# Attention and a max-of-three MLP on one core: DVE takes over the first weight conversions, the hidden layer is split batch by batch, and the queues of the first loads change

## The chip, the cores and the metric

The kernel runs on one core of a Trainium2 chip. Five engines work side by side, each through its own queue of instructions in order: TensorE (PE, with its weight loads, PEld, shown apart), VectorE (DVE), ScalarE (ACT), GpSimd (POOL) and SyncE (SP, which here only issues DMAs). They meet through semaphores. The metric is the device time of one execution in microseconds, and the time of a kernel is the median of its runs.

## What is computed

Twelve heads of attention with a soft cap on the scores, for four batches of 448 tokens, and after it a layer with a maximum over three products:

```python
scores = q @ k.T / sqrt(64)                 # (4, 12, 448, 64) each
scores = cap * tanh(scores / cap)
attn = exp(scores - max); attn = attn / (sum(attn) + 1e-9)
x = heads side by side of attn @ v          # (1792, 768)
h = maximum(maximum(x @ w1, x @ w2), x @ w3)
out = h @ w_out                             # weights 768 x 768, given in 64 bits
```

## The kernel before

**Attention.** The 48 pairs of batch and head go in twelve steps t = 0 to 11 of four heads each (two PE row halves by two column halves). A step has seven key blocks j. For each j, `scores(t, j)` is four products on PE into one of two PSUM tiles `qk`, `tanh(t, j)` (ACT, from PSUM to one of ten tiles `e_t`) and `expo(t, j)` (ACT, in place) follow, `add(t, j)` sums the exponentials on DVE into `s_t`, and `values(t, j)` multiplies by v on PE into `av`. At the start of step t + 1, `sums(t)` adds over the keys by a product with ones on PE into `sm`, `recip(t)` transposes, inverts and transposes back on DVE, `normalize(t)` multiplies `av` by the result on DVE, which frees `av` for `values(t + 1, 0)`, and `split_x(t)` writes x as a high part `xh` and a rest `xl`, both float32r. The two `qk` tiles are used in turn, so `scores(t + 1, 2)` waits until `tanh(t + 1, 0)` has read its tile. In steps 0 to 3 and 11 (`BY_PE`) the last block's exponentials are added by a second product in `sums`, in the others by `add(t, 6)` on DVE.

**Weights.** `conv(n, i)` makes weight tile n (128 x 768, of 24) from its 64-bit form `wd` in steps i: a scaled copy of the upper word on ACT, three integer operations on DVE over `cw`, a cast to `wh` on ACT and the rest to `wl` on DVE. `CONV` says after which attention step which parts stand; they are written between `scores(t + 1, 1)` and `expo(t, 6)`.

**The layer.** `products(n, b, ...)` is eighteen products, `xh wh`, `xl wh`, `xh wl` for six blocks. Eight of the 96 groups (n, b) are done inside attention, one in each of steps 4 to 11 (`FILL`), ahead of `scores(t, 5)`. The other 88 run in `mlp` after it: n = 0 to 17 give the three products of each hidden block, `empty` copies the first to `m_t` (ACT) and takes the maximum with the others (DVE); n = 18 to 23 are the output, copied by ACT and sent by SP. Between n = 17 and n = 18, `split_h(b, f)` writes h as high part and rest over `xh` and `xl`: a cast on ACT and a subtraction on DVE for each of 24 pairs (b, f).

The order on every engine is the order of the code (`tc.manual_schedule()`); waits come from the tiles.

Of the kernel before, what the change touches and what calls it, by code (L numbers as in the profile page):

```python
# [31 lines left out]
CONV = {0: [(0, k) for k in range(5)], 1: [(1, 0), (1, 1)], 2: [(1, 2), (1, 3), (1, 4)],  # L32
        4: [(2, 0), (2, 1)], 5: [(2, 2), (2, 3), (2, 4)], 9: [(3, 0)], 10: [(3, 1)], 11: [(3, 2)]}
FIRST_CONV = 3
# [3 lines left out]
def attn_max_mlp_kernel(ctx: ExitStack, tc: tile.TileContext, q, k, v, cap, wts, out):  # L38
# [28 lines left out]
    r_t = ring("r_t", 2, [128, 2 * QB])  # L67
    xh = ring("xh", B, [128, KC, S], F32R)
# [124 lines left out]
    def conv(n, step):  # L193
# [3 lines left out]
        if step == 0:  # L197
            nc.scalar.activation(out=d, in_=top.bitcast(F32), func=AF.Copy, scale=2.0 ** -112)
            nc.vector.tensor_scalar(
                out=w, in0=w, scalar1=3, scalar2=1, op0=ALU.logical_shift_left, op1=ALU.bitwise_or  # L200
            )
        elif step == 1:
# [3 lines left out]
        elif step == 2:  # L206
# [3 lines left out]
        elif step == 3:  # L210
            nc.scalar.copy(out=h, in_=d)  # L211
        else:
            tt(nc.vector, l, d, h.bitcast(F32), ALU.subtract)
# [10 lines left out]
    def empty(n, b, ps):  # L224
        if n >= 3 * KC:
            o = o_t[outs[0] % len(o_t)]
            outs[0] += 1
            nc.scalar.copy(out=o, in_=ps)
            nc.sync.dma_start(out=out[n - 3 * KC, b], in_=o)
            return  # L230
# [12 lines left out]
    def step(t, eps):  # L243
        last = t - 1
        if t:
            sums(last, last in BY_PE)
            recip(last, eps)
            values(last, 3)
        if t < NG:
            tanh(t, 1)  # L250
            expo(t, 0)
            scores(t, 3)
# [3 lines left out]
        if t < NG:  # L256
            tanh(t, 2)
            expo(t, 1)
            add(t, 1)
            scores(t, 4)  # L260
# [3 lines left out]
        if t < NG:  # L264
            tanh(t, 3)
            expo(t, 2)
            add(t, 2)
# [69 lines left out]
    def mlp(done, convs):  # L337
# [14 lines left out]
        if fast:  # L352
# [6 lines left out]
            for n in range(2):  # L359
# [124 lines left out]
```

## Time and profile before

| | us |
|---|---|
| median of 3 runs (lowest, highest) | 559.41 (553.05, 559.76) |
| profiled execution, its own time | 559.23 |
| profiled execution, span from first to last instruction | 557.2 |
| PE busy in the span | 518.9 |
| DVE busy | 257.9 |
| ACT busy | 235.2 |

The time of the profiled execution is 2.0 us more than its span. A matmul counts as busy from its issue to its end and the next starts before that, so a busy PE may still be paced by something. DVE and ACT are busiest in the first part, the attention, which ends near 213 us; from there PE runs one stream of products. "idle before" in a row is what the engine waited just ahead of it, and the arrow names what ended the wait.

### The profile page before, as it was taken

The page shows a single profiled execution, that of the slowest core. Times are in us where ns is not written, and L with a number is a line of the kernel's source. Part 1 is how long each engine was busy: PE and PEld are TensorE (multiplying, and loading weights), DVE is VectorE, ACT ScalarE, POOL GpSimd, SP SyncE. Part 2 cuts the span into 40 slices and gives each one's busy share as a digit, 9 for nine tenths or more (in the row PEclk, how much of TensorE's full clock was granted, in tenths as well). Part 3 has the DMA queues.
Part 4 walks back from the last instruction along what each step waited for, and adds up shares of the span by engine and source line. Part 5 has one row for each costly group of instructions (what it writes and reads, how often), then busy time and mean ns, then how long its engine had stood idle before and what let it go on. Part 6 is the DMA issues. An engine that isn't in the chain of part 4 may idle for free.

```text
span 557.2 us, 7444 instructions
## 1 busy us (share of the span) xinstructions
PE 518.9 (93%) x3217; PEld 383.8 (69%) x3217; DVE 257.9 (46%) x325; ACT 235.2 (42%) x291; POOL 1.1 (0%) x7
## 2 busy tenths in 40 slices
PE   6598699899999999999999999999999978999997
PEld 2133234454444447999999999999999957999996
DVE  1578577867677884513323323332332366211200
ACT  5788698768978870311121031020111172222211
POOL 0000000000000000000000000000000000000000
PEclk9899899989999999999999999999999986999999
DMA  7322043213243201111111111020130100333111
GB/s 250 127 86 85 31 156 100 100 34 100 72 151 101 89 1 58 58 56 58 56 58 56 58 56 43 27 102 0 58 101 13 58 0 34 107 122 124 67 51 70
DMA packets 12311, 41.44 MB, mean 74 GB/s; under 512 B 1392, under 2 KB 4592, under 8 KB 12272
## 3 DMA queue, kind: packets, MB, share of 16 engines
q1 hardware_dynamic: 12240, 40.90, 21.5%
q8 instruction: 27, 0.44, 0.3%
q14 instruction: 12, 0.10, 0.1%
q0 software_dynamic: 32, 0.00, 0.0%
HBM read 35.39 MB, written 5.51 MB: 73 GB/s over the span
## 4 chain that ended last, share of the span: by engine, by line
PE 80%; ACT 12%; DVE 5%; issue 1%; ACTq 0%; DVEq 0%
PE qk L219 10%; PE qk L218 10%; PE qk L220 10%; PE sm L218 7%; PE qk L117 7%; PE sm L220 7%; PE sm L219 7%; ACT e_t L123 6%; PE av L131 6%; PE av L218 5%; PE av L220 5%; ACT e_t L126 5%; PE av L219 5%; PE sm L145 3%; DVE xl L95 2%; DVE s_t L95 1%
## 5 line engine op out<-in xcount | busy, mean ns | idle before, releaser
L219 PE MATMUL qk<-xl,wh 128*128 128x448 f32 x264 | 99.8, 378 | 6.0 <-DVE xl L95 6.0
L117 PE MATMUL qk<-q_t,k_t 64*64 64x448 f32 x672 | 81.8, 560 | 25.1 <-ACT e_t L123 24.7
L220 PE MATMUL qk<-xh,wl 128*128 128x448 f32 x264 | 98.9, 375 | 0.0
L218 PE MATMUL qk<-xh,wh 128*128 128x448 f32 x264 | 98.9, 375 | 0.0
L123 ACT ACTIVATE e_t<-qk,sc_t 128x896 f32<-128x896 f32 x84 | 83.0, 1002 | 23.2 <-PE qk L117 22.1
L126 ACT ACTIVATE e_t<-e_t,acap 128x896 f32<-128x896 f32 x84 | 86.3, 1038 | 0.4
L211 ACT CAST wh<-cw 128x768 fp32r<-128x768 f32 x24 | 20.0, 834 | 136.4 <-DVE cw L207 136.4
L131 PE MATMUL av<-e_t,v_t 64*64 64x448 f32 x672 | 75.9, 538 | 1.4 <-DVE x_t L95 1.4
L117 PEld LDWEIGHTS qk<-q_t,k_t 64*64 64x64 f32 x672 | 23.3, 135 | 67.8 <-ACT e_t L123 40.9
L218 PE MATMUL sm<-xh,wh 128*128 128x448 f32 x180 | 67.0, 372 | 0.0
L220 PE MATMUL sm<-xh,wl 128*128 128x448 f32 x180 | 66.2, 368 | 0.0
L219 PE MATMUL sm<-xl,wh 128*128 128x448 f32 x180 | 66.1, 367 | 0.0
L95 DVE TENSOR_TENSOR s_t<-s_t,e_t 128x896 f32<-128x896 f32 x55 | 59.9, 1088 | 11.5 <-ACT e_t L126 10.0
L219 PEld LDWEIGHTS qk<-xl,wh 128*128 128x128 f32 x264 | 50.5, 191 | 14.0 <-DVE xl L95 9.2
L218 PEld LDWEIGHTS qk<-xh,wh 128*128 128x128 f32 x264 | 50.8, 193 | 6.0 <-issue 0.7
L220 PEld LDWEIGHTS qk<-xh,wl 128*128 128x128 f32 x264 | 50.7, 192 | 5.1
L131 PEld LDWEIGHTS av<-e_t,v_t 64*64 64x64 f32 x672 | 25.5, 134 | 40.5 <-issue 36.8
L218 PE MATMUL av<-xh,wh 128*128 128x448 f32 x132 | 48.6, 368 | 0.0
L219 PE MATMUL av<-xl,wh 128*128 128x448 f32 x132 | 48.6, 368 | 0.0
L220 PE MATMUL av<-xh,wl 128*128 128x448 f32 x132 | 48.6, 368 | 0.0
L95 DVE TENSOR_TENSOR wl<-cw,wh 128x768 fp32r<-128x768 f32 x24 | 22.9, 955 | 51.3 <-ACT wh L211 51.3
L218 PEld LDWEIGHTS sm<-xh,wh 128*128 128x128 f32 x180 | 33.8, 188 | 8.8 <-DVE s_t L95 5.6
(62 smaller groups left out, 417.3 us busy)
## 6 DMA issues: line engine op xcount, KB each, us to landing
wd<-in_wts_dram SPq DMA_DIRECT2D x24, 768.0 KB, 4.4
q_t<-in_q_dram SPq DMA_DIRECT2D x12, 448.0 KB, 4.3
v_t<-in_v_dram SPq DMA_DIRECT2D x12, 448.0 KB, 3.2
k_t<-in_k_dram SPq DMA_DIRECT2D x11, 448.0 KB, 3.4
out_dram<-q_t SPq DMA_DIRECT2D x8, 224.0 KB, 2.0
out_dram<-s_t SPq DMA_DIRECT2D x8, 224.0 KB, 1.9
out_dram<-x_t SPq DMA_DIRECT2D x8, 224.0 KB, 2.2
k_t<-in_k_dram SPq DMA_DIRECT2D x1, 320.0 KB, 6.5
```

The source lines that it names most:

```text
L95: eng.tensor_tensor(out=out, in0=in0, in1=in1, op=op)
L117: nc.tensor.matmul(ps[rows(s), R, 0:S], k_t[t % 2][rows(R), j, s, :], q_t[t % 2][rows(R), s, :], start=True, stop=True, skip_group_check=True,
L123: nc.scalar.activation(out=e_of(t, j), in_=slot(t, j)[:, :, 0:S], func=AF.Tanh, scale=sc_t)
L126: nc.scalar.activation(out=e_of(t, j), in_=e_of(t, j), func=AF.Exp, scale=acap)
L131: nc.tensor.matmul(av[rows(R), s, 0:S], v_t[t % 2][rows(s), j, R, :], e_of(t, j)[rows(s), R, :], start=(j == 0), stop=(j == NJ - 1), skip_ ...
L145: nc.tensor.matmul(sm[rows(R), s, 0:S], ones[rows(s), :], part[rows(s), R, :], start=(i == 0), stop=(i == len(parts) - 1), skip_group_chec ...
L211: nc.scalar.copy(out=h, in_=d)
L218: nc.tensor.matmul(ps, w_h, a_h, start=(kc == 0), stop=False)
L219: nc.tensor.matmul(ps, w_h, a_l, start=False, stop=False)
L220: nc.tensor.matmul(ps, w_l, a_h, start=False, stop=(kc == KC - 1))
```

## The change

Six edits. (1) `conv` has six steps: the scaled copy and the first integer operation are now separate. In steps 0 and 4 of it the engine is DVE, unless `by_act` is set; tile 0, tile 1 and the cast of tile 2 go to DVE, tile 2's and tile 3's scaled copies stay on ACT (`SCALED`), and all tiles of `mlp` keep ACT. Tile 0's first four parts stand behind single adds of step 0; the other parts are spread over steps 1 to 5, 9 and 10, and stand behind all adds of their step. (2) `values(t, 3)` moves from behind `sums(t)` to ahead of `scores(t + 1, 2)`; in steps without a fill, `scores(t, 6)` comes ahead of `values(t, 0)`. (3) `split_h` is done for batch b right behind group (17, b). (4) The first q load and cap go to ACT's queue, cap from POOL's. (5) The last output tile is emptied in two halves, by DVE and ACT, and sent by SP and ACT. (6) A tile `pad` of 128 bytes per partition stands ahead of x and the weights and moves them. The loads of q and k stand earlier in their step and those of `wd` inside the steps; SP's queue keeps the order of q, k and v.

```diff
-CONV = {0: [(0, k) for k in range(5)], 1: [(1, 0), (1, 1)], 2: [(1, 2), (1, 3), (1, 4)],
-        4: [(2, 0), (2, 1)], 5: [(2, 2), (2, 3), (2, 4)], 9: [(3, 0)], 10: [(3, 1)], 11: [(3, 2)]}
+CONV = {1: [(0, 4), (0, 5)], 2: [(1, 0), (1, 1)], 3: [(1, 2), (1, 3)], 4: [(1, 4), (1, 5), (2, 1)],
+        5: [(2, 2), (2, 3), (2, 4), (2, 5)], 9: [(3, 1)], 10: [(3, 2), (3, 3)]}
+SCALED = {4: 2, 9: 3}
+LOADS = {0: 1, 2: 2, 6: 3, 11: 4}
...
     r_t = ring("r_t", 2, [128, 2 * QB])
+    tl("pad", [128, 32])
     xh = ring("xh", B, [128, KC, S], F32R)
...
-    def conv(n, step):
+    def conv(n, step, by_act=False):
...
-        if step == 0:
+        if step == 0 and by_act:
             nc.scalar.activation(out=d, in_=top.bitcast(F32), func=AF.Copy, scale=2.0 ** -112)
+        elif step == 0:
+            nc.vector.tensor_scalar_mul(d, top.bitcast(F32), 2.0 ** -112)
+        elif step == 1:
...
-        elif step == 3:
+        elif step == 4 and by_act:
             nc.scalar.copy(out=h, in_=d)
+        elif step == 4:
+            nc.vector.tensor_copy(out=h, in_=d)
...
+            if (n, b) == (NU - 1, B - 1):
+                one, two = slice(0, S // 2), slice(S // 2, S)
+                nc.vector.tensor_copy(out=o[:, one], in_=ps[:, one])
+                nc.sync.dma_start(out=at[:, one], in_=o[:, one])
+                nc.scalar.copy(out=o[:, two], in_=ps[:, two])
+                nc.scalar.dma_start(out=at[:, two], in_=o[:, two])
+                return
...
     def step(t, eps):
         last = t - 1
+        if 0 < t < NG - 1:
+            load_qk(t + 1)
         if t:
             sums(last, last in BY_PE)
             recip(last, eps)
-            values(last, 3)
...
+        if t in SCALED:
+            conv(SCALED[t], 0, True)
         add(t, 3)
+        if t == 0:
+            conv(0, 0)
+            conv(0, 1)
         scores(t, 5)
-        values(t, 0)
-        tanh(t, 5)
         if not fill:
+            tanh(t, 5)
             expo(t, 4)
+            scores(t, 6)
+            values(t, 0)
+        else:
+            values(t, 0)
+            tanh(t, 5)
+            scores(t, 6)
         add(t, 4)
-        scores(t, 6)
+        if t == 0:
+            conv(0, 2)
...
         add(t, 5)
+        if t == 0:
+            conv(0, 3)
         if t + 1 < NG:
             scores(t + 1, 1)
-        for n, i in CONV.get(t, []):
-            conv(n, i)
         expo(t, 6)
         if t not in BY_PE:
             add(t, 6)
+        for n, i in CONV.get(t, []):
+            conv(n, i)
+        values(t, 3)
         if t + 1 < NG:
             tanh(t + 1, 0)
             scores(t + 1, 2)
...
-                if n == 3 * KC - 1 and b == B - 1:
+                if n == 3 * KC - 1:
                     for f in range(KC):
-                        for bb in range(B):
-                            split_h(bb, f)
+                        split_h(b, f)
...
-        nc.gpsimd.dma_start(out=cap_t, in_=cap.partition_broadcast(128))
         nc.sync.dma_start(out=k_t[0][:, 0:2].rearrange("p a b c -> p (a b c)"), in_=k[0, :, 0:256])
-        nc.sync.dma_start(out=flat(q_t[0]), in_=q[0])
+        nc.scalar.dma_start(out=flat(q_t[0]), in_=q[0])
+        nc.scalar.dma_start(out=cap_t, in_=cap.partition_broadcast(128))
```

Three places show what that does to the queues. DVE at the end of step 0, before: the adds of step 0 (`s_t_86`), then tile 0's conversion in one piece (`cw_106`), then `recip` of step 0 (`STREAM_TRANSPOSE`).

```order
L95 TENSOR_TENSOR s_t_86<-s_t_86,e_t_79 128x896
L95 TENSOR_TENSOR s_t_86<-s_t_86,e_t_80 128x896
L95 TENSOR_TENSOR s_t_86<-s_t_86,e_t_81 128x896
L199 TENSOR_SCALAR cw_106<-cw_106 128x768
L203 SCALAR_TENSOR_TENSOR cw_106<-wd_104,cw_106 128x768
L207 SCALAR_TENSOR_TENSOR cw_106<-wd_104,cw_106 128x768
L95 TENSOR_TENSOR wl_111<-cw_106,wh_108 128x768
L152 STREAM_TRANSPOSE x_t_88<-sm 128x896
```

The same place on DVE with the change (`cw_107` is the same tile):

```order
L97 TENSOR_TENSOR s_t_86<-s_t_86,e_t_79 128x896
L202 TENSOR_SCALAR cw_107<-wd_105 128x768
L204 TENSOR_SCALAR cw_107<-cw_107 128x768
L97 TENSOR_TENSOR s_t_86<-s_t_86,e_t_80 128x896
L208 SCALAR_TENSOR_TENSOR cw_107<-wd_105,cw_107 128x768
L97 TENSOR_TENSOR s_t_86<-s_t_86,e_t_81 128x896
L212 SCALAR_TENSOR_TENSOR cw_107<-wd_105,cw_107 128x768
L154 STREAM_TRANSPOSE x_t_88<-sm 128x896
```

The scaled copy is now DVE's, the parts stand between the adds, and the cast and the rest have left step 0. PE at the border of steps 1 and 2, before: `scores(2, 0)`, `values(1, 2)`, `scores(2, 1)`, `scores(2, 2)`, the two products of `sums(1)`, `values(1, 3)` (`e_t_76`), `scores(2, 3)`.

```order
L117 MATMUL qk_117<-q_t_70,k_t_72 64x448 x4
L131 MATMUL av<-e_t_85,v_t_75 64x448 x4
L117 MATMUL qk_118<-q_t_70,k_t_72 64x448 x4
L117 MATMUL qk_117<-q_t_70,k_t_72 64x448 x4
L145 MATMUL sm<-s_t_87,ones 64x448 x4
L145 MATMUL sm<-e_t_79,ones 64x448 x4
L131 MATMUL av<-e_t_76,v_t_75 64x448 x4
L117 MATMUL qk_118<-q_t_70,k_t_72 64x448 x4
```

The same place on PE with the change:

```order
L119 MATMUL qk_118<-q_t_70,k_t_72 64x448 x4
L133 MATMUL av<-e_t_85,v_t_75 64x448 x4
L119 MATMUL qk_119<-q_t_70,k_t_72 64x448 x4
L133 MATMUL av<-e_t_76,v_t_75 64x448 x4
L119 MATMUL qk_118<-q_t_70,k_t_72 64x448 x4
L147 MATMUL sm<-s_t_87,ones 64x448 x4
L147 MATMUL sm<-e_t_79,ones 64x448 x4
L119 MATMUL qk_119<-q_t_70,k_t_72 64x448 x4
```

`values(1, 3)` has moved three places up, ahead of the block that waits for `tanh(2, 0)`. DVE around the split of h, before: maxima of groups (17, 1) to (17, 3) with parts of tile 19's conversion, then the subtractions, block by block over all batches (`xl_96` is batch 0).

```order
L95 TENSOR_TENSOR e_t_84<-e_t_84,av 128x448
L203 SCALAR_TENSOR_TENSOR cw_107<-wd_105,cw_107 128x768
L95 TENSOR_TENSOR e_t_85<-e_t_85,sm 128x448
L207 SCALAR_TENSOR_TENSOR cw_107<-wd_105,cw_107 128x768
L95 TENSOR_TENSOR e_t_85<-e_t_85,av 128x448
L95 TENSOR_TENSOR wl_112<-cw_107,wh_109 128x768
L95 TENSOR_TENSOR xl_96<-m_100,xh_92 128x448
L95 TENSOR_TENSOR xl_97<-m_101,xh_93 128x448
L95 TENSOR_TENSOR xl_98<-m_102,xh_94 128x448
L95 TENSOR_TENSOR xl_99<-m_103,xh_95 128x448
L95 TENSOR_TENSOR xl_96<-e_t_76,xh_92 128x448
```

The same place on DVE with the change, from the maximum of group (17, 0) on (`xl_97` is batch 0 here):

```order
L97 TENSOR_TENSOR e_t_84<-e_t_84,sm 128x448
L204 TENSOR_SCALAR cw_108<-cw_108 128x768
L97 TENSOR_TENSOR xl_97<-m_101,xh_93 128x448
L97 TENSOR_TENSOR xl_97<-e_t_76,xh_93 128x448
L97 TENSOR_TENSOR xl_97<-e_t_78,xh_93 128x448
L97 TENSOR_TENSOR xl_97<-e_t_80,xh_93 128x448
L97 TENSOR_TENSOR xl_97<-e_t_82,xh_93 128x448
L97 TENSOR_TENSOR xl_97<-e_t_84,xh_93 128x448
L97 TENSOR_TENSOR e_t_84<-e_t_84,av 128x448
L208 SCALAR_TENSOR_TENSOR cw_108<-wd_106,cw_108 128x768
L97 TENSOR_TENSOR xl_98<-m_102,xh_94 128x448
```

All six subtractions of a batch now stand ahead of the next batch's maximum.

## Rows read from the trace of the kernel before

**Rows 1.** The page: granted TensorE clock in 40 slices; shares of the chain by engine

```profile
PEclk9899899989999999999999999999999986999999
...
PE 80%; ACT 12%; DVE 5%; issue 1%; ACTq 0%; DVEq 0%
```

**Rows 2.** Timeline of ACT: start, duration, instruction, idle before; x2 is tanh(t, 0) and tanh(t, 1)

```profile
8.30 1.91 ACT L123 ACTIVATE e_t<-qk,sc_t 128x896 f32<-128x896 f32 x2 [0.51 <-DVE eps_f L408]
...
25.57 1.89 ACT L123 ACTIVATE e_t<-qk,sc_t 128x896 f32<-128x896 f32 x2
...
41.64 1.90 ACT L123 ACTIVATE e_t<-qk,sc_t 128x896 f32<-128x896 f32 x2
...
74.83 1.89 ACT L123 ACTIVATE e_t<-qk,sc_t 128x896 f32<-128x896 f32 x2
...
92.38 1.88 ACT L123 ACTIVATE e_t<-qk,sc_t 128x896 f32<-128x896 f32 x2
...
128.08 1.89 ACT L123 ACTIVATE e_t<-qk,sc_t 128x896 f32<-128x896 f32 x2
...
193.16 1.89 ACT L123 ACTIVATE e_t<-qk,sc_t 128x896 f32<-128x896 f32 x2
```

**Rows 3.** The chain that ended last, step 0 to step 1: start, time, piece

```profile
19.34 0.94 ACT e_t L126
...
23.88 0.83 ACT wh L211
...
26.61 1.77 PE qk L117 x8
```

**Rows 4.** The same chain in step 5 and in step 7 (fill: sm)

```profile
99.67 0.40 PE sm L218
...
103.52 0.96 PE qk L117 x8
...
130.85 0.75 PE av L131 x8
...
135.36 0.41 PE sm L218
...
139.27 0.96 PE qk L117 x8
```

**Rows 5.** One window, step 7: busy us (count) of PE, PEld, DVE, ACT, POOL; clock

```profile
128.08:144.22 16.14, 15.56 (x146) 7.69 (x138) 11.77 (x13) 13.78 (x17) 0.00 (x0) 1.00 0.26 85
```

**Rows 6.** Groups by form on DVE: count, busy us, mean ns, idle before

```profile
L95 DVE TENSOR_TENSOR s_t<-s_t,e_t 128x896 f32<-128x896 f32 x55 | 59.9, 1088 | 11.5 <-ACT e_t L126 10.0
L203 DVE SCALAR_TENSOR_TENSOR cw<-wd,cw 128x768 int32<-128x768 int32 x24 | 23.0, 957 | 0.5
...
L199 DVE TENSOR_SCALAR cw<-cw 128x768 int32<-128x768 int32 x24 | 13.4, 556 | 40.9 <-ACT cw L198 40.9
...
L167 DVE CAST xh<-x_t 128x896 fp32r<-128x896 f32 x12 | 7.4, 620 | 0.0
```

**Rows 7.** Timeline of PE and DVE: first products of groups (18, 0), (18, 2), (23, 3); the split

```profile
451.54 0.37 PE L218 MATMUL qk<-xh,wh 128*128 128x448 f32 x1
...
455.29 10.79 DVE L95 TENSOR_TENSOR xl<-e_t,xh 128x448 fp32r<-128x448 f32 x20
...
471.11 0.37 PE L218 MATMUL qk<-xh,wh 128*128 128x448 f32 x1
...
549.23 0.37 PE L218 MATMUL av<-xh,wh 128*128 128x448 f32 x1
```

**Rows 8.** Timeline and one window (5 to 9 us): start and end of the program

```profile
5.22 1.90 PE L117 MATMUL qk<-q_t,k_t 64*64 64x448 f32 x16
...
7.35 0.20 ACT L400 ACTIVATE acap<-cap_t 128x1 f32<-128x1 f32 x1 [5.33 <-DMA cap_t<-in_cap_dram]
...
553.19 0.53 ACT L228 COPY x_t<-av 128x448 f32<-128x448 f32 x1 [3.19 <-PE av L220]
...
5.00:9.00 4.00, 2.02 (x17) 0.65 (x16) 0.60 (x5) 1.11 (x3) 0.00 (x0) 1.00 0.81 307
```

More of the change, by code (lines that the diff above doesn't have):

```diff
@@ L31 @@
 BY_PE = (0, 1, 2, 3, 11)
-CONV = {0: [(0, k) for k in range(5)], 1: [(1, 0), (1, 1)], 2: [(1, 2), (1, 3), (1, 4)],
-        4: [(2, 0), (2, 1)], 5: [(2, 2), (2, 3), (2, 4)], 9: [(3, 0)], 10: [(3, 1)], 11: [(3, 2)]}
-FIRST_CONV = 3
+CONV = {1: [(0, 4), (0, 5)], 2: [(1, 0), (1, 1)], 3: [(1, 2), (1, 3)], 4: [(1, 4), (1, 5), (2, 1)],
+        5: [(2, 2), (2, 3), (2, 4), (2, 5)], 9: [(3, 1)], 10: [(3, 2), (3, 3)]}
+SCALED = {4: 2, 9: 3}
+LOADS = {0: 1, 2: 2, 6: 3, 11: 4}
 @with_exitstack
@@ L201, in conv @@
             )
-        elif step == 1:
+        elif step == 2:
             nc.vector.scalar_tensor_tensor(
@@ L205, in conv @@
             )
-        elif step == 2:
+        elif step == 3:
             nc.vector.scalar_tensor_tensor(
@@ L227, in empty @@
             outs[0] += 1
+            at = out[n - 3 * KC, b]
+            if (n, b) == (NU - 1, B - 1):
[5 more added lines that the diff above has]
+                return
             nc.scalar.copy(out=o, in_=ps)
-            nc.sync.dma_start(out=out[n - 3 * KC, b], in_=o)
+            nc.sync.dma_start(out=at, in_=o)
             return
@@ L247, in step @@
             recip(last, eps)
-            values(last, 3)
[L249 to L252, printed above, removed]
+        if t == NG:
+            for j in range(4, NJ):
+                values(last, j)
+            normalize(last)
+            split_x(last)
+            return
+        fill = FILL.get(t)
+        tanh(t, 1)
+        expo(t, 0)
+        scores(t, 3)
         if t:
@@ L255, in step @@
             values(last, 5)
[L256 to L260, printed above, removed]
+        tanh(t, 2)
+        expo(t, 1)
+        add(t, 1)
+        scores(t, 4)
         if t:
@@ L263, in step @@
             normalize(last)
[L264 to L267, printed above, removed]
+        tanh(t, 3)
+        expo(t, 2)
+        add(t, 2)
         if t:
@@ L270, in step @@
         if 0 < t < NG - 1:
-            load_qk(t + 1)
             load_v(t + 1)
-        if t == NG:
-            return
-        fill = FILL.get(t)
+        if t in LOADS:
+            conv_load(LOADS[t])
         if fill:
@@ L363, in mlp @@
                 if n == 0:
-                    for i in (3, 4):
-                        conv(3, i)
+                    for i in (4, 5):
+                        conv(3, i, True)
         for n in range(NU):
@@ L373, in mlp @@
                     for i in convs[b]:
-                        conv(n + 2, i)
+                        conv(n + 2, i, True)
                 elif n == 2 and b == B - 1:
-                    for i in range(5):
-                        conv(4, i)
+                    for i in range(6):
+                        conv(4, i, True)
                 elif not fast and n == 0 and b == B - 1:
-                    for i in (3, 4):
-                        conv(3, i)
-                if n == 3 * KC - 1 and b == B - 1:
+                    for i in (4, 5):
+                        conv(3, i, True)
+                if n == 3 * KC - 1:
                     for f in range(KC):
-                        for bb in range(B):
-                            split_h(bb, f)
-    convs = [(0,), (1,), (2, 3), (4,)]
+                        split_h(b, f)
+    convs = [(0, 1), (2,), (3, 4), (5,)]
     with tc.manual_schedule():
-        nc.gpsimd.dma_start(out=cap_t, in_=cap.partition_broadcast(128))
         nc.sync.dma_start(out=k_t[0][:, 0:2].rearrange("p a b c -> p (a b c)"), in_=k[0, :, 0:256])
-        nc.sync.dma_start(out=flat(q_t[0]), in_=q[0])
+        nc.scalar.dma_start(out=flat(q_t[0]), in_=q[0])
+        nc.scalar.dma_start(out=cap_t, in_=cap.partition_broadcast(128))
         nc.sync.dma_start(out=k_t[0][:, 2:].rearrange("p a b c -> p (a b c)"), in_=k[0, :, 256:])
@@ L416, in attn_max_mlp_kernel @@
             load_v(1)
-            conv_load(1)
             for t in range(NG + 1):
                 step(t, eps_f)
-                if t in (3, 8):
-                    conv_load(2 if t == 3 else 3)
-                if t == NG - 1:
-                    conv_load(4)
             mlp({*FILL.values()}, convs)
@@ L429, in attn_max_mlp_kernel @@
             for n in range(3):
-                for i in range(5):
+                for i in range(6):
                     conv(n, i)
-                if n < 3:
-                    conv_load(n + 2)
-            for i in range(3):
+                conv_load(n + 2)
+            for i in range(4):
                 conv(3, i)
```

## The prediction, made before the result was known

> **What bounds the kernel now.** I read the chain that ended last first. Its shares are PE 80%, ACT 12% and DVE 5% [rows 1], but they average over two stages. In the layer PE alone sets the time: from the first product of group (18, 2) to that of (23, 3) lie 78.12 us for 378 products, 206.7 ns each, so a group of eighteen takes 3.72 us [rows 7]. No edit removes products, so the 88 groups outside attention stay near 327 us, and the gain must come from places where this stream stops and from attention. Next the timeline of ACT, for the lengths of the steps [rows 2]: step 0 takes 17.27 us, step 1 16.07, steps 2 and 3 together 33.19, step 4 17.55, steps 5 and 6 together 35.70, steps 7 to 10 together 65.08. The floor for a step on ACT is known from step 0: from the first tanh to the sixth exp start [rows 2, 3] twelve operations take 11.04 us, 0.92 us each, so fourteen take 12.9 us. On the mean every step is 3 to 5 us above that. The chain shows two reasons.
>
> The first is the conversion. In step 0 ACT has issued its last but one exp at 19.34; the cast of the first weight tile stands ahead of the last exp in its queue and runs at 23.88, when DVE has done its part, and PE's next scores come at 26.61, at 1.77 us for what takes 0.96 to 0.98 elsewhere [rows 3, 4]: the granted clock had fallen to its lower level, 1.2 GHz, behind that idle time (the slices below 9) [rows 1]. The second is the fill. In step 7 eighteen products stand from 135.36 to 139.27 between values and scores(t, 5) [rows 4]; PE is busy 15.56 of 16.14 us, DVE only 11.77 [rows 5]. PE's chain from tanh(t, 0) to scores(t, 5) sets that step, and 0.75 us of it is values(t - 1, 3) at 130.85 [rows 4].
>
> **The split of h.** The first product of (18, 0) starts at 451.54 and that of (18, 2) at 471.11 [rows 7]: 19.57 us for two groups that need 7.44, because each block of PE waits for subtractions that DVE makes for all four batches in turn; part of the loss is the low clock that follows. With the change DVE does six subtractions per batch, at 10.79 / 20 = 0.54 us each [rows 7]. Per batch that is 3.2 us, a maximum of some 0.6 us, and up to 0.96 us of conversion [rows 6]: 4.8 us against 3.72 on PE. DVE starts 3.9 us into group (17, 0) and ends four batches at 3.9 + 19.3 = 23.2 us; PE wants batch 3 at seven groups, 26.0 us, and batch 0 at 14.9 us, when it has been ready since 8.7. All of it is covered: **-12.1 us**. If the cover failed, what comes back is the wait for batch 3 first.
>
> **Conversions of tiles 0 to 3.** ACT loses the copies and casts that stood ahead of its exps. DVE gains a scaled copy and a cast per tile. No row has the scaled copy on DVE: it reads every second word. A contiguous TENSOR_SCALAR takes 0.56, an operation that reads the same strided words 0.96 [rows 6]; I take 0.56 to 0.96 and the middle, since it is one operand like the former and strided like the latter. The cast is 0.62 us for 896 columns [rows 6], about 0.55 for 768. In step 0 four parts cost 0.76 + 0.56 + 2 x 0.96 = 3.2 us on DVE (3.0 to 3.4) beside five adds of 1.09 in 12.9 us: covered, and the last add still ends about 14.1 us after the step's start, while sums wants it at 12.9 + 1.8. Step 0 falls to 12.9: **-4.4**.
>
> In steps 1 to 3 ACT's floor is 12.9, plus 0.2 for scores(t, 4), which come 0.75 sooner than before because of values(t, 3) (next part). DVE there has step 7's 11.77 less one add, 10.7 us [rows 5, 6], and 1.5 to 1.9 of conversion: 12.2 to 12.6 and some gaps against 13.1. That is the thinnest cover of the change. The parts stand behind all adds and ahead of recip, which waits for PE's sums anyway. I take 13.1 each: step 1 **-3.0**, which includes the end of its slow-clock stretch, steps 2 and 3 **-7.0**.
>
> Fill steps: step 4 loses 0.75 by values and the scaled copy that stood late in it, but gets one behind the empty of its fill, where 0.4 us of it meet scores(t, 5): 16.4, **-1.15**. Step 5's cast no longer waits; the step is the fill step of 16.1 less 0.75, 15.3. Its four parts (3.4 us) push recip of step 6 by 2 us, but the fill wants sm only 6.5 us into the step, and at most 0.3 remains: 15.7. Steps 5 and 6 **-4.7**, the rest of their low-clock stretch included.
>
> **values(t, 3).** In its new place PE works while it would wait for tanh(t + 1, 0) (0.6 us in step 7: 16.14 less 15.56), and 0.75 us leaves the chain behind sums [rows 4, 5]. Steps 7 to 10 go to 15.4 each, step 9 without the ACT copy that now lies in the fill's wait: 65.08 to 61.6, **-3.5**. Step 11 gains the 0.75 and as much at its end, where values(11, 3) covers sums' wait: **-1.5**. Steps without a fill have scores(t, 6) ahead of values(t, 0), which waits for normalize in any case: 0.
>
> **Start and end.** The first tanh at 8.30 is 0.95 behind cap's landing at 7.35 [rows 2, 8]. On ACT's queue cap follows q. q lets scores start at 5.22 [rows 8]. If q had the engines to itself the first tanh could be at 6.3, -2.0. If it shares them with k and v, some 448 KB go beside it, at 307 GB/s [rows 8] 1.5 us: scores at 6.7, cap right behind, tanh at 7.6, -0.7. If cap's small pieces are slow on that queue it could be +0.7. I take **-0.7**, the shared case, as SP has four loads waiting.
>
> The Trainium skill speaks against more than that: "DMA: Bandwidth & Descriptors", section "Issuing engines are not separate DMA queues", says that transfers from all engines run on the same 16 DMA engines and interleave, and that issuing from several saves only the time to issue. By that rule the shared case holds and the sum is 521; with q alone it would be 519.7. No trace so far has two queues loading at once, so the run must tell.
>
> The last copy (0.53 at 553.19 [rows 8]) is halved on two engines: **-0.2**. Moving x and the weights: rows show eighteen products in 3.91 us in step 7 and 3.85 in step 5 [rows 4], with the same tiles as later groups at 3.72 to 3.73 steady, so the place shows no price: 0. The other queue edits keep the order of SP's loads, which land long ahead: 0.
>
> **Sum.** -12.1 - 4.4 - 3.0 - 7.0 - 1.15 - 4.7 - 3.5 - 1.5 - 0.7 - 0.2 = -38.25. From the profiled execution's 559.23 that gives **521 us**; it lies 0.2 under the median of the three runs, whose lowest is 6 us away.
>
> **Rivals.** (a) DVE becomes the bound of steps 0 to 6. For: cover of half a microsecond. Against: the parts stand where DVE waited. If half of what it gets there, 3.2 + 1.6 + 1.5 + 1.9 + 2.1 + 3.5 = 13.8, comes onto the chain, 528; if all, 535. (b) The split stays in the way: DVE's queue is in order, and were a batch needing 8 us instead of 4.8 (casts on ACT waiting for the conversion's cast), batch 3 would be late by 10: 531. Against: the cast's wait is one of four parts. (c) The new place of x and the weights changes the products' pace. The difference of step 5 and step 7 is 0.06 us in eighteen, 3.3 ns; over 1584 products 5.3 us: 515.5 if faster, 526 if slower. (d) On the other side, slower than before: the same mechanism, with a pace above 206.7 + 38.25 / 1584 = 230.8 ns, for instance weight loads no longer hidden; at 250 ns the time is 521 + 69 = 590. It decides only above 230.8, and no warm group in the trace is near it. (e) The change doesn't do what it says at one place, as if values(t, 3) only moved the wait to the next tanh: 0.75 us come back in each of steps 1 to 11, 8.25, 529. For: tanh(t + 1, 0) is late in every step. Against: in step 7 it leaves 0.6 us of idle time on PE [rows 5].
>
> **How the numbers follow.** My forecast has 0.64, (a) 0.14, (b) 0.04, (c) 0.10, (d) 0.02, (e) 0.06. The terms' own bounds: start -2.0 to +0.7, strided copy 0.4, steps 1 to 3 by 0.5 each, together some 4 us either way. The range reaches down to the faster (c) with a good start, 513, and up to (a) whole less a part, 531. A measurement of this kernel tells about 2%, 11 us, from no change. Faster by over 2% means under 548: all but (d) and part of what I haven't seen: 0.95; the same 0.03; slower 0.02.
>
> **What would show it.** Right: the PE gap between (18, 0) and (18, 2) gone, 7.4 us apart; no slice of low clock in the middle of attention and near the end; no cast of weights on ACT in steps 0 to 5; steps 0 to 3 near 13 us and 7 to 10 near 15.4; first tanh near 7.6. Wrong: sums waiting for DVE's adds or products for recip in steps 1 to 6, casts of h on ACT behind one another so that (18, 3) starts late, or a product pace other than 206.7 ns.

## The result and the profile after

The changed kernel takes 522.39 us (median of four runs, 521.95 to 522.64); the kernel before took 556.23 in the same set (551.82 to 559.76). The ratio is 0.9395 with an interval of [0.9308, 0.9481]. The forecast was 521 within 513 to 531. It was worked out from the profiled execution of the kernel before, 559.23, where it says 38.25 us less; between the two profiled executions it is 36.9, between the two medians 33.8, since the runs of the kernel before are spread over 8 us.

The profiled execution took 522.36 us (before: 559.23), its span 520.2 us (557.2). The page of the kernel after, granted clock by slice and shares of the chain by engine, stands against [rows 1]:

```profile
PEclk8999999999999999999999999999999999999999
...
PE 88%; ACT 7%; DVE 2%; issue 1%; ACTq 0%; DVEq 0%
```

ACT's share fell from 12% to 7%, DVE's from 5% to 2%. The slices under 9 in the middle of attention and near the end are gone; one is left at the start. The timeline of ACT, kernel after, against [rows 2, 3] (each line of L125 is the first tanh of a step; 19.45 is the last two exps of step 0):

```profile
8.55 1.91 ACT L125 ACTIVATE e_t<-qk,sc_t 128x896 f32<-128x896 f32 x2 [0.50 <-DVE eps_f L439]
...
19.45 2.00 ACT L128 ACTIVATE e_t<-e_t,acap 128x896 f32<-128x896 f32 x2
21.32 1.93 ACT L125 ACTIVATE e_t<-qk,sc_t 128x896 f32<-128x896 f32 x2
...
34.38 1.90 ACT L125 ACTIVATE e_t<-qk,sc_t 128x896 f32<-128x896 f32 x2
...
60.44 1.90 ACT L125 ACTIVATE e_t<-qk,sc_t 128x896 f32<-128x896 f32 x2
...
76.91 1.89 ACT L125 ACTIVATE e_t<-qk,sc_t 128x896 f32<-128x896 f32 x2
...
107.62 1.89 ACT L125 ACTIVATE e_t<-qk,sc_t 128x896 f32<-128x896 f32 x2
...
169.12 1.89 ACT L125 ACTIVATE e_t<-qk,sc_t 128x896 f32<-128x896 f32 x2
```

The exps of step 0 run on without a break and step 1 begins right behind them. Before, the last but one ended at 20.28 [rows 3] and the last began here (timeline of ACT, kernel before):

```profile
24.62 1.04 ACT L126 ACTIVATE e_t<-e_t,acap 128x896 f32<-128x896 f32 x1
```

Between them lay 4.3 us with two pieces of conversion. Two windows of the kernel after, step 2 and step 7 (busy us and count of PE, PEld, DVE, ACT, POOL; clock), the second against [rows 5]:

```profile
34.38:47.41 13.03, 12.26 (x132) 4.71 (x128) 12.02 (x15) 12.90 (x16) 0.00 (x0) 1.00 0.35 121
...
107.62:123.11 15.49, 15.49 (x146) 7.58 (x142) 12.40 (x14) 13.66 (x17) 0.00 (x0) 1.00 0.27 89
```

A step without a fill is now ACT's (12.90 of 13.03 us busy), one with a fill PE's (15.49 of 15.49). The timeline of PE, kernel after, first products of groups (18, 0), (18, 2) and (23, 3), against [rows 7]:

```profile
426.02 0.37 PE L225 MATMUL qk<-xh,wh 128*128 128x448 f32 x1
...
433.46 0.37 PE L225 MATMUL qk<-xh,wh 128*128 128x448 f32 x1
...
511.58 0.37 PE L225 MATMUL av<-xh,wh 128*128 128x448 f32 x1
```

(18, 0) and (18, 2) are 7.44 us apart, where it was 19.57; from (18, 2) to (23, 3) it is 78.12 us in both kernels. At the two ends nothing was gained. The timeline of the kernel after, start and end, against [rows 8]:

```profile
5.04 2.59 PE L119 MATMUL qk<-q_t,k_t 64*64 64x448 f32 x16
...
7.61 0.20 ACT L431 ACTIVATE acap<-cap_t 128x1 f32<-128x1 f32 x1 [4.68 <-DMA cap_t<-in_cap_dram]
...
515.56 0.39 DVE L238 COPY x_t<-av 128x224 f32<-128x224 f32 x1 [31.28 <-PE av L227]
...
515.98 0.34 ACT L240 COPY x_t<-av 128x224 f32<-128x224 f32 x1 [3.62 <-DVE x_t L238]
```

ACT can read cap at 7.61 against 7.35. ACT's half copy doesn't run beside DVE's: it waits for it (515.98, released by DVE). From the first product of the last group to the end of the span it is 8.6 us, where it was 8.0.

The span, term by term from these rows and those of before. A step lasts from its first tanh to that of the next, step 11 to the first product of the layer (213.37 before, 187.84 after); the stretches of the layer that the table leaves out are equally long in both kernels:

| term | predicted | measured |
|---|---|---|
| start, to the first tanh | -0.7 | 8.30 to 8.55: +0.25 |
| step 0 | -4.4 | 17.27 to 12.77: -4.50 |
| step 1 | -3.0 | 16.07 to 13.06: -3.01 |
| steps 2 + 3 | -7.0 | 33.19 to 26.06: -7.13 |
| step 4 | -1.15 | 17.55 to 16.47: -1.08 |
| steps 5 + 6 | -4.7 | 35.70 to 30.71: -4.99 |
| steps 7 to 10 | -3.5 | 65.08 to 61.50: -3.58 |
| step 11 | -1.5 | 20.21 to 18.72: -1.49 |
| split of h | -12.1 | 19.57 to 7.44: -12.13 |
| end | -0.2 | 8.0 to 8.6: +0.6 |
| sum | -38.25 | -37.0 (spans 557.2 to 520.2) |

### The profile page after: what moved, and what is told of

Read it like the earlier page. It is cut to its first block, busy times and chain, and to the rows that moved or that the text cites. A ratio compares the mean times of both kernels' runs of the same rounds, so it can differ in the third digit from the quotient of the medians.

```text
span 520.2 us, 7463 instructions
## 1 busy us (share of the span) xinstructions
PE 507.7 (98%) x3217; PEld 380.7 (73%) x3217; DVE 258.7 (50%) x331; ACT 230.0 (44%) x286; POOL 0.4 (0%) x6
## 4 chain that ended last, share of the span: by engine, by line
PE 88%; ACT 7%; DVE 2%; issue 1%; ACTq 0%; DVEq 0%
PE qk L225 11%; PE qk L227 11%; PE qk L226 10%; PE qk L119 8%; PE av L133 8%; PE sm L225 7%; PE sm L227 7%; PE sm L226 7%; PE av L227 5%; PE av L226 5%; PE av L225 5%; ACT e_t L125 3%; ACT e_t L128 3%; PE sm L147 3%; DVE x_t L154 1%
## 5 line engine op out<-in xcount | busy, mean ns | idle before, releaser
L225 PE MATMUL qk<-xh,wh 128*128 128x448 f32 x264 | 97.3, 368 | 0.0
L227 PE MATMUL qk<-xh,wl 128*128 128x448 f32 x264 | 97.2, 368 | 0.0
L226 PE MATMUL qk<-xl,wh 128*128 128x448 f32 x264 | 97.1, 368 | 0.0
L125 ACT ACTIVATE e_t<-qk,sc_t 128x896 f32<-128x896 f32 x84 | 83.2, 1006 | 11.8 <-PE qk L119 10.7
L133 PE MATMUL av<-e_t,v_t 64*64 64x448 f32 x672 | 74.8, 536 | 0.0
L216 ACT CAST wh<-cw 128x768 fp32r<-128x768 f32 x21 | 17.5, 835 | 120.9 <-DVE cw L212 120.9
L225 PEld LDWEIGHTS qk<-xh,wh 128*128 128x128 f32 x264 | 49.6, 188 | 5.6 <-issue 0.7
L227 PEld LDWEIGHTS qk<-xh,wl 128*128 128x128 f32 x264 | 49.6, 188 | 5.0
L225 PEld LDWEIGHTS sm<-xh,wh 128*128 128x128 f32 x180 | 33.8, 188 | 8.7 <-DVE x_t L157 4.9
```

Source lines behind the costliest of these rows:

```text
L125: nc.scalar.activation(out=e_of(t, j), in_=slot(t, j)[:, :, 0:S], func=AF.Tanh, scale=sc_t)
L133: nc.tensor.matmul(av[rows(R), s, 0:S], v_t[t % 2][rows(s), j, R, :], e_of(t, j)[rows(s), R, :], start=(j == 0), stop=(j == NJ - 1), skip_ ...
L225: nc.tensor.matmul(ps, w_h, a_h, start=(kc == 0), stop=False)
L226: nc.tensor.matmul(ps, w_h, a_l, start=False, stop=False)
L227: nc.tensor.matmul(ps, w_l, a_h, start=False, stop=(kc == KC - 1))
```

## The experiments

Unless it says otherwise a kernel is the changed one with the edit shown, and medians are set against 522.39. The sets ran on several chips, and the median of the kernel before was 554.07 to 560.03 in them, so a difference of about 1 us between two sets is not shown by the medians alone.

**h split for all batches together.**

```diff
-                if n == 3 * KC - 1:
+                if n == 3 * KC - 1 and b == B - 1:
                     for f in range(KC):
-                        split_h(b, f)
+                        for bb in range(B):
+                            split_h(bb, f)
```

> The changed kernel with one part undone: h is split for all four batches together, after group (17, 3). Theory (the wait for all twenty subtractions and the low clock behind it cost 12.1 us): 522.4 + 12.1 = 534.5 us, (18, 0) and (18, 2) some 19.6 us apart, a stretch at the lower clock behind the gap. Rival (the part was over-sized, since the rest of the change has altered what DVE and ACT have queued there): under 528 us.

Measured: 533.15 us (532.70 to 533.73), 10.8 more. The timeline of PE, h together:

```profile
425.89 0.37 PE L225 MATMUL qk<-xh,wh 128*128 128x448 f32 x1
...
434.60 0.74 PE L226 MATMUL qk<-xl,wh 128*128 128x448 f32 x1 [0.65 <-DVE xl L97]
435.13 0.57 PE L227 MATMUL qk<-xh,wl 128*128 128x448 f32 x1
...
436.74 0.74 PE L226 MATMUL qk<-xl,wh 128*128 128x448 f32 x1 [0.65 <-DVE xl L97]
...
444.42 0.36 PE L225 MATMUL qk<-xh,wh 128*128 128x448 f32 x1
...
521.03 0.36 PE L225 MATMUL av<-xh,wh 128*128 128x448 f32 x1
```

Every 2.14 us PE gets one block (436.74 less 434.60), the time of four subtractions of 0.54, and its products take 0.57 where they took 0.37: the granted clock is at its lower level, 1.2 GHz, in the records from 428.29 to 441.95. The gap from (18, 0) to (18, 2) is 18.53, 11.1 more than 7.44. The theory holds, with 10.8 for its 12.1. The net loss is smaller than the gap because (18, 2) to (23, 3) now takes 76.61 us, not 78.12: behind the stop the products came 202.7 ns apart instead of 206.7. That was in no theory, and the last two experiments follow it.

**The kernel before with this part alone** (the reverse edit in the kernel before).

> The kernel before with one part of the change alone: h is split batch by batch behind the last groups of tile 17. Theory (the gap and the low clock behind it cost 10.8 to 12.1 us whatever stands ahead of them): 10.8 to 12.1 us under the kernel before on the same chip, 546 to 549 us, with (18, 0) and (18, 2) 7.4 us apart. Rival (the gain needs the new order of the conversion's parts between the groups, which this kernel has not got): less than 8 us, with casts of h on ACT that wait.

Measured: 541.68 us (541.40 to 547.99) against 555.32 for the kernel before in the same set; ratio 0.9766 [0.9696, 0.9836]; that is 13.6 less, more than the theory's 10.8 to 12.1. The timeline of PE, h alone, groups (18, 0) and (18, 2):

```profile
447.64 0.37 PE L218 MATMUL qk<-xh,wh 128*128 128x448 f32 x1
...
454.94 0.36 PE L218 MATMUL qk<-xh,wh 128*128 128x448 f32 x1
```

7.30 us apart: the gap closes without the rest of the change, and the rival falls. The size of the gain is not clean here: in this execution the products of the layer came 202.7 ns apart from its first group on, which is worth some 6 us, and the runs of the kernel before spread over 8 us (552.41 to 560.40) for which no trace gives the reason.

**Conversions put back.**

```diff
-CONV = {1: [(0, 4), (0, 5)], 2: [(1, 0), (1, 1)], ...
-SCALED = {4: 2, 9: 3}
+CONV = {0: [(0, k) for k in range(6)], 1: [(1, 0), (1, 1), (1, 2)], 2: [(1, 3), (1, 4), (1, 5)],
+        4: [(2, 0), (2, 1), (2, 2)], 5: [(2, 3), (2, 4), (2, 5)], 9: [(3, 0), (3, 1)], 10: [(3, 2)], 11: [(3, 3)]}
...
+        for n, i in CONV.get(t, []):
+            conv(n, i, True)
         expo(t, 6)
         if t not in BY_PE:
             add(t, 6)
-        for n, i in CONV.get(t, []):
-            conv(n, i)
```

> The changed kernel with the conversions of tiles 0 to 3 put back as they were: scaled copies and casts on ACT, all ahead of the last exp of steps 0, 1, 2, 4, 5, 9, 10 and 11; the place of values(t, 3) and the loads stays. Theory (the conversion on ACT is what made steps 0 to 6 long): of the terms, 4.4 for step 0, 3.0 for step 1, 7.0 for steps 2 and 3, 0.4 for step 4 and 3.2 for steps 5 and 6, together 18.0: 540 us, with stretches at the lower clock back near 23 and 60 us. Rival (the place of values and of the sixth scores did most of it in steps 1 to 6): only step 0 gets longer, 527 to 530 us.

Measured: 538.14 us (537.48 to 538.72), 15.8 more. The timeline of ACT, conversions back, steps 0 and 2:

```profile
20.16 0.95 ACT L199 ACTIVATE cw<-wd 128x768 f32<-128x768 f32 x1
23.91 0.83 ACT L215 CAST wh<-cw 128x768 fp32r<-128x768 f32 x1 [2.79 <-DVE cw L211]
24.64 1.04 ACT L127 ACTIVATE e_t<-e_t,acap 128x896 f32<-128x896 f32 x1
25.59 1.88 ACT L124 ACTIVATE e_t<-qk,sc_t 128x896 f32<-128x896 f32 x2
...
56.20 0.83 ACT L215 CAST wh<-cw 128x768 fp32r<-128x768 f32 x1 [3.24 <-DVE cw L211]
```

The cast waits 2.79 and 3.24 us for DVE with the last exp behind it; the lower clock level is back in the records from 25.93 to 29.34 and from 56.65 to 63.47. Step 0 is 17.27 us long again, to the hundredth; steps 1 to 6 are 15.16, 17.13, 15.26, 16.75, 17.17 and 15.33, and step 9 is 0.73 longer. The theory holds; it was 2.2 too high, chiefly because step 6 loses nothing and step 1 only 2.1. The edit puts back two things at once, the engine of the copies and casts and their place ahead of the last exp. How much the place alone would give, with the copies and casts still on ACT but behind that exp, was not run.

**values(t, 3) back behind the sums.**

```diff
             recip(last, eps)
+            values(last, 3)
...
-        values(t, 3)
         if t + 1 < NG:
             tanh(t + 1, 0)
```

> The changed kernel with values(t, 3) back in its old place, behind the sums of the next step. Theory (0.75 us leave the chain of each step in which PE is the bound): 0.75 in each of the eight fill steps, 0.4 in each of steps 1 to 3, 7.2 in all, 529.6 us; a fill step goes from 15.35 to 16.1. Rival (values only moves the wait, so its place is worth nothing): 522.4 us, with the fill steps at 15.35 to 15.5.

Measured: 531.21 us (one run of four at 524.98, the others 531.17 to 531.29), 8.8 more. The timeline of ACT, values back, the starts of steps 7 and 8:

```profile
112.13 1.89 ACT L125 ACTIVATE e_t<-qk,sc_t 128x896 f32<-128x896 f32 x2
...
128.27 1.88 ACT L125 ACTIVATE e_t<-qk,sc_t 128x896 f32<-128x896 f32 x2
```

Step 7 takes 16.14, exactly as before [rows 2]; steps 1 to 3 take 13.81, 13.78 and 13.78, also some 0.75 more each where 0.4 was expected. Over steps 1 to 10 the loss is 0.65 to 0.76 each, and rival (e) falls.

**Conversion twice.** DVE's parts behind the adds of steps 1, 2, 3 and 5 are made a second time.

```diff
-CONV = {1: [(0, 4), (0, 5)], 2: [(1, 0), (1, 1)], 3: [(1, 2), (1, 3)], 4: ...
-        5: [(2, 2), (2, 3), (2, 4), (2, 5)], ...
+CONV = {1: 2 * [(0, 4), (0, 5)], 2: 2 * [(1, 0), (1, 1)], 3: 2 * [(1, 2), (1, 3)], 4: ...
+        5: 2 * [(2, 2), (2, 3), (2, 4), (2, 5)], ...
```

> The changed kernel with DVE's conversion parts behind the adds of steps 1, 2, 3 and 5 made twice (the second time on the same data, so the tiles hold the same): 1.5, 1.1, 1.9 and 3.4 us more on DVE. Theory (DVE has idle time left of 0.6 to 1.3 us a step there, and what goes beyond reaches sums or the fill): 1.0 us for step 2, 0 to 0.3 for step 3, 1.0 for step 4, 1.5 for step 6, together 2 to 4 us: 524.4 to 526.4. Rival (the cover is thick, since only values of the second half of a step wait for recip): 522.4 to 522.9. Second rival (DVE is already the bound of these steps): all 7.9 us, 530.

Measured: 527.61 us (526.60 to 528.58), 5.2 more. Steps 1 and 2 keep 13.05 and 13.03, step 3 takes 13.66 in place of 13.03 and step 6 takes 21.02 in place of 15.33. The timeline of PE, conversion twice, in step 3 and in step 6:

```profile
49.52 0.98 PE L147 MATMUL sm<-s_t,ones 64*64 64x448 f32 x8 [0.40 <-DVE s_t L97]
...
98.26 0.93 PE L133 MATMUL av<-e_t,v_t 64*64 64x448 f32 x8
101.98 0.74 PE L225 MATMUL sm<-xh,wh 128*128 128x448 f32 x1 [2.78 <-DVE x_t L154]
102.52 0.57 PE L226 MATMUL sm<-xl,wh 128*128 128x448 f32 x1
```

The fill waits 2.78 us for recip's transpose to empty sm, the clock falls at the end of that wait (1.2 GHz in the records from 101.35 to 108.17), and the eighteen products, 0.37 apart instead of 0.21, cost about as much again (2.8 us). In steps 1 to 3 the cover is some 2 us over two steps: the 1.5 us of step 1 cost nothing by themselves, DVE carries them over, and with the 1.1 of step 2 the last add comes 0.40 late for sums in step 3; the 1.9 of step 3 cost step 4 less than 0.1. DVE is not the bound. The theory's steps were wrong on both sides: 1.0, 0 to 0.3, 1.0 and 1.5 us for steps 2, 3, 4 and 6 came out as 0, 0.63, 0.06 and 5.69, and in the fill step of this execution the clock doubled the wait. Of the other three runs two, with a mean granted clock of 0.997 and 1.000 where this one has 0.989, took 526.93 and 526.60 us where it took 528.28: there the clock seems not to have fallen, which no trace shows.

**Start and end, three ways.** First loads as before:

```diff
+        nc.gpsimd.dma_start(out=cap_t, in_=cap.partition_broadcast(128))
         nc.sync.dma_start(out=k_t[0][:, 0:2] ...
-        nc.scalar.dma_start(out=flat(q_t[0]), in_=q[0])
-        nc.scalar.dma_start(out=cap_t, in_=cap.partition_broadcast(128))
+        nc.sync.dma_start(out=flat(q_t[0]), in_=q[0])
```

> The changed kernel with the first loads as before: cap first on POOL's queue, q second on SP's. Theory (cap's landing sets the first tanh in both kernels, and on ACT's queue behind q it lands later): the first tanh goes from 8.55 back to 8.3 us, first scores at 5.2, 522.1 us. Rival (the first tanh waits for q's and k's scores, and the new queue for q is a gain that something else hid): the first tanh at 8.9 or later, 522.9 us. The two lie within what the times can tell; the first tanh in the trace decides.

Measured: 522.01 us (521.28 to 522.08); first tanh at 7.79, half a microsecond sooner than the theory's 8.3, first scores at 5.28. Cap's landing, not q's, sets the first tanh here too. Then cap on POOL's queue with q left on ACT's, and the special case for the last tile taken out of `empty`:

> The changed kernel with two edits at its ends, read apart in the trace: cap on POOL's queue while q stays on ACT's, and the last output tile copied whole by ACT and sent in one piece. Theory for the start (cap's landing sets the first tanh, q on ACT's queue is worth nothing): first tanh at 7.8 to 8.3 us, against 8.3 to 8.6 with cap behind q. Rival for the start (q's place sets it): 8.5. Theory for the end (ACT's half copy waits until DVE's is done, and half a tile lands no sooner than a whole one, so the split costs): from the first product of the last group to the end of the span 8.0 us in place of 8.6. Rival for the end (the split gains, and the end is longer for another reason): 8.8. In time 521.4 by the theories, 522.6 by the rivals.

Measured: 521.17 us (521.05 to 521.28). The timeline of ACT, cap on POOL and last tile whole:

```profile
7.04 0.20 ACT L424 ACTIVATE acap<-cap_t 128x1 f32<-128x1 f32 x1 [4.58 <-DMA cap_t<-in_cap_dram]
...
7.98 1.91 ACT L125 ACTIVATE e_t<-qk,sc_t 128x896 f32<-128x896 f32 x2 [0.51 <-DVE eps_f L432]
...
514.88 0.53 ACT L236 COPY x_t<-av 128x448 f32<-128x448 f32 x1 [3.18 <-PE av L227]
```

First tanh at 7.98, and from the last group's first product (510.92) to the end of the span 8.1 us: both numbers are those of the theories. For the end every trace agrees (7.9 to 8.1 us in the six kernels that copy the last tile whole, 8.5 to 8.7 in the eight that halve it). For the start a single trace decides little: the first tanh is at 8.30, 8.37 and 7.79 in the three traces with the old first loads, and at 8.07 to 8.63 in the five others with the new ones. Third, cap ahead of q on ACT's queue, and for the second half of the last tile another tile (`p = o_t[outs[0] % len(o_t)]`):

> The changed kernel with two other edits at its ends: cap ahead of q on ACT's queue, and the second half of the last output tile in a tile of its own. Theory for the start (cap's small pieces are slow because they share the engines with q, k, v and the weights): cap lands before 5 us and the first tanh waits for scores instead, at 6.5 to 7 us. Rival (the pieces take some 6 us from their issue in any place): first tanh at 8.0 or later. Theory for the end (the two halves share one tile, and that is why ACT waits for DVE): the copies run beside each other and the end is 8.2 us. Rival (they read one bank of results, and that makes ACT wait): as before, 8.6.

Measured: 522.61 us (521.82 to 523.37). The DMA issues of this kernel (KB each, us from issue to landing) and its timeline:

```profile
q_t<-in_q_dram ACTq DMA_DIRECT2D x1, 448.0 KB, 6.0
...
cap_t<-in_cap_dram ACTq DMA_DIRECT2D x1, 0.5 KB, 3.6
```

```profile
4.35 0.20 ACT L432 ACTIVATE acap<-cap_t 128x1 f32<-128x1 f32 x1 [1.42 <-DMA cap_t<-in_cap_dram]
...
7.26 2.52 PE L119 MATMUL qk<-q_t,k_t 64*64 64x448 f32 x12 [2.15 <-DMA q_t<-in_q_dram]
...
516.82 0.34 ACT L241 COPY q_t<-av 128x224 f32<-128x224 f32 x1 [3.62 <-DVE x_t L238]
```

cap lands early, but q behind it needs 6.0 us (4.0 in the changed kernel), so the first tanh comes at 9.09: the theory was right on cap and wrong on the tanh. With two tiles ACT still waits for DVE, so the shared tile was not the reason; what the two kernels still have in common is the bank of `av` that both halves read. The Trainium skill, "PSUM — Partial Sum Buffer", section "PSUM bank collisions raise a hardware error", says that two engines must not read one bank in the same partitions at once and must be ordered by semaphores; the wait in this row, which DVE's copy ends, agrees. That the copies would run beside each other out of two banks wasn't tried.

**No pad.** The line `tl("pad", [128, 32])` is taken out.

> The changed kernel without the 128 bytes that move the tiles of x and the weights. Theory (their place shows no price): 522.4 us within 0.5, products 206.7 ns apart in the layer. Rival (the place sets the products' pace): 5 us more or less, with another pace in all groups of the layer.

Measured: 522.22 us (521.70 to 522.49), products 206.7 ns apart: the tiles' place is worth nothing.

**Both ends put together**: cap alone on ACT's queue, q on SP's, last tile whole.

> The changed kernel with its two ends put together from what the runs showed: cap alone on ACT's queue, q second on SP's, and the last output tile copied whole and sent in one piece. Theory (cap's small pieces land 3.6 us after their issue if nothing is ahead of them, and q lands at 5.2 us if it isn't behind them): acap near 4.4, first scores near 5.3, first tanh near 6.2 us, and 8.1 us from the first product of the last group to the end: 2.3 and 0.5 us less than the changed kernel, 519.5 us. Rival (cap's pieces hold up q and k on any queue, since they share the engines): first scores at 6.5 us or later, first tanh at 7.5 or later, 521 us.

Measured: 521.36 us (519.69 to 522.12, six runs). The timeline, cap alone on ACT's queue:

```profile
4.20 0.20 ACT L424 ACTIVATE acap<-cap_t 128x1 f32<-128x1 f32 x1 [1.75 <-DMA cap_t<-in_cap_dram]
...
5.69 2.30 PE L119 MATMUL qk<-q_t,k_t 64*64 64x448 f32 x16 [0.58 <-DMA q_t<-in_q_dram]
...
7.31 1.90 ACT L125 ACTIVATE e_t<-qk,sc_t 128x896 f32<-128x896 f32 x2 [2.68 <-PE qk L119]
```

cap lands as the theory has it; but now the first tanh waits for scores, which start at 5.69 and need 1.6 us, so the start gains 1.2 us on the changed kernel, not 2.3. Neither text has the start right: the scores come between the theory's 5.3 and the rival's 6.5. The median is no better than with cap on POOL's queue (521.17) and misses the theory's 519.5; the profiled execution, at 520.27, is among the fastest of six, and why the others are longer stays open.

**A short product between the groups**, in that last kernel:

```diff
             ps = bank()
+            if b == 0:
+                nc.tensor.matmul(ps[:, 0:64], wh[n % 3][:, 0, :], xh[b][:, 0, 0:64], start=True, stop=True)
             products(n, b, ps, range(KC))
```

> The kernel with cap alone on ACT's queue and the last tile whole, and one more short product of 64 columns ahead of the first group of each of the 24 tiles, into a bank that the group then writes afresh (nothing of the output changes). In the traces the products of a group are 206.7 ns apart in some stretches and some 202.6 in others; a stream that does not stop keeps its pace, and stretches behind a stop have either. Theory (a break in the even row of products lets the pace be drawn anew): groups of both kinds, on the mean 2 to 3 us less and some 1 us more for the added products, 517 to 519 us. Rival (the break changes nothing): 206.7 ns in every group and 520.5 us.

Measured: 517.61 us (516.44 to 517.83, six runs) against 521.36 beside it. Only 21 of the 24 tiles get the short product, because the first groups of tiles 0 to 2 lie in attention. In the trace the first groups of the layer are 3.72 us apart; from the first short product on every group's products are 202.6 ns apart, none goes back. The time is the theory's; the groups are not, since all of them have the lower spacing and not both. With one short product only (`if (n, b) == (3, 0)`):

> The kernel with cap alone on ACT's queue, the last tile whole, and one short product of 64 columns in the whole layer, ahead of the first group of tile 3 (nothing of the output changes). With one ahead of each tile all groups from there on were 202.6 ns a product, and a tile's first group cost some 0.08 us for its break. Theory (one break moves the row to the lower pace, and the row keeps it until it stops): 84 groups of 18 products at 4.1 ns less, 6.2 us, from 521.4: 515.2 us in every run, 3.65 us from group to group. Rival (each break draws anew, and the runs with 21 breaks only had many draws): some runs near 515 and some near 521. Second rival (the lower pace must be renewed by each break): near 521 us.

Measured: 515.25 us (514.12 to 515.96, five runs), ratio to the kernel before 0.9292 [0.9264, 0.932]. The timeline of PE, one short product, first products of the group ahead of it, the group behind it (198.68, 202.43), the next one, (18, 2) and (23, 3):

```profile
198.68 0.37 PE L225 MATMUL qk<-xh,wh 128*128 128x448 f32 x1
...
202.43 0.44 PE L225 MATMUL sm<-xh,wh 128*128 128x448 f32 x1
...
206.14 0.37 PE L225 MATMUL av<-xh,wh 128*128 128x448 f32 x1
...
428.68 0.36 PE L225 MATMUL qk<-xh,wh 128*128 128x448 f32 x1
...
505.28 0.36 PE L225 MATMUL av<-xh,wh 128*128 128x448 f32 x1
```

From (18, 2) to (23, 3) 76.60 us for 378 products, 202.6 ns each, against 78.12 and 206.7. The theory's 515.2 stands, and all five runs lie within 2 us of each other: one break is enough. The set ran on another chip than the two before it, where the kernel before took 554.07 and not 555.32, so the 6 us rest on the spacing in the traces more than on the two medians. This is the fastest kernel of the study.

## Why the prediction was right, point by point

**The split** was the largest term and met within 0.1 us. Undoing it brings the gap, the wait for DVE's subtractions and the low clock back; done alone it closes the gap as well. Undone one at a time the split, the conversions and values cost 10.8, 15.8 and 8.8 us, 35.4 together, against the 37.0 between the two spans.

**Conversions.** Steps 0 to 6 came out within 0.3 us each. The form rows of DVE, kernel after, give the two prices that [rows 6] could only bound:

```profile
L218 DVE CAST wh<-cw 128x768 fp32r<-128x768 f32 x3 | 1.7, 554 | 0.0
L202 DVE TENSOR_SCALAR cw<-wd 128x768 f32<-128x768 f32 x2 | 1.1, 560 | 0.0
```

The cast was put at 0.55. The scaled copy that reads every second word was taken as 0.76 and is 0.56, the lower bound: beside the 0.556 of the contiguous TENSOR_SCALAR [rows 6] the stride costs this operation next to nothing. The cover that the prediction called the thinnest, half a microsecond a step, is nearer to one, as the doubled parts show; rival (a), DVE as the bound, is excluded for the kernel as it is. (In steps 1 to 3 the chain that ended last does run through recip on DVE, but ACT is idle for only 0.13 us of step 2, so DVE can cost no more than that in it.) What DVE's taking over is worth apart from the new place of the parts is argued, not shown.

**values(t, 3)** has its 0.75 us. The prediction set down the gain of steps 1 to 3 under the conversions, without a share for values; there the runs have 2.3 us lost with values put back and 8.4 with the conversions put back, against the 10.1 that the three steps lost in all. The new order of scores(t, 6), which was put at nothing, was not undone by itself.

**Start and end: the two terms that did not come.** "I take **-0.7**, the shared case" failed at its price and at its path. By that case q would let scores start at 6.7; they start at 5.04, and the first tanh waits for cap, not for q. The DMA issues of the two kernels (KB each, us from issue to landing), the first line before, the others after:

```profile
cap_t<-in_cap_dram POOLq DMA_DIRECT2D x1, 0.5 KB, 6.1
...
q_t<-in_q_dram ACTq DMA_DIRECT2D x1, 448.0 KB, 4.0
...
cap_t<-in_cap_dram ACTq DMA_DIRECT2D x1, 0.5 KB, 6.4
```

cap is as slow behind q as it was on POOL's queue. The prediction has it "right behind" q, though cap's landing sets the first tanh in [rows 8] too; nor is it so that no trace had two queues loading at once, since POOL's and SP's do in the kernel before. The case "if cap's small pieces are slow on that queue" came nearest: +0.25 where +0.7 was allowed, and by the spread above the traces don't tell +0.25 from nothing. The rule of the Trainium skill that the prediction cites ("DMA: Bandwidth & Descriptors", section "Issuing engines are not separate DMA queues") agrees in that q gains little by its new queue: it lands 4.0 to 4.5 us after its issue there, unless cap is ahead of it, and at a median of 4.3 on SP's. It says nothing of the small pieces. The halving of the last copy, put at **-0.2**, failed because the halves follow each other, 0.76 us to the end of the second where the whole copy takes 0.53, and half a tile lands 2.1 to 2.8 us after its issue, a whole one at a median of 1.9 to 2.3. Together the two terms are some 1.8 us above the forecast; steps 0 to 11 and the split came out 0.6 us better.

**Rival (c)** asked the right question with the wrong cause. The 3.3 ns between the products of two fill steps was no price of an address, since taking the pad out changes nothing; the row of products has two paces, and in the traces without a short product it keeps the one with which it starts. Here the prediction had luck that it could not know of: its starting point, 559.23, is an execution at 206.7 ns, and the changed kernel ran at 206.7 ns as well. Had one of them had the other pace, as the layer of the run with h alone did, the measured change would have been some 6 us off the sum with every term of it right.

## What to carry to other kernels

An engine that is half idle is not thereby free to help: look for the instruction behind which the critical engine's own work is queued, and move that, into a place where the helping engine waits anyway. Price a wait on PE with the lower clock that follows it: in the fill step of "conversion twice" it cost 2.8 us behind a wait of 2.78, and with the conversions back step 3, in which no conversion stands, is 2.2 us longer. And before calling an even row of matmuls the floor, compare its spacing in several stretches and runs: here a single short product was worth 6 us by the spacing in its trace.

## What was not expected of the hardware

**Two paces of one row of products.** 448-column products with a weight load each come 206.7 ns apart in one stretch and 202.6 in another of the same program, at the same granted clock of 1.0. Fill groups, which start after a stop, show both within one trace; the uninterrupted layer keeps the pace it starts with; one 64-column product moved it from the slower to the faster in each of eleven runs, as far as their times tell, and in both that have a trace. In no trace did a running row go the other way. At 4.1 ns a product the layer differs by 6 us between them, which is the distance of the single runs at 524.98 and 547.99 above from their neighbours; that those runs differ by this is argued from the size, since they have no trace. Why the row keeps one of the two stays open. The Trainium skill, "TensorE: Matmul & The Clock Gate", section "Back-to-back issue gap", gives columns / 2.4 + 2.5 ns for an isolated product at the full clock, an estimate of 189 ns for 448 columns, and some 131 ns a product for a sustained row of weight loads and products of 512 columns. Neither pace agrees with either figure, and the measurement decides.

**A 512-byte load can be the slowest of all.** cap, 4 bytes into each of 128 partitions, needed 3.4 to 3.6 us from its issue as the first load on ACT's queue, 5.6 to 6.2 on POOL's queue, where nothing is ahead of it either, and 5.9 to 6.5 behind q. In the one trace in which q is queued behind it, q took 6.0 us, where it takes 4.0 to 4.5 ahead of it. Why POOL's queue is slower for it stays open.
